# Two attention blocks in one program: new orders for the first block, and its later value loads cut into four

## The chip, the cores and the metric

The kernel runs on one core of a Trainium2 chip. The core has TensorE (PE; its weight loads are shown apart as PEld), VectorE (DVE), ScalarE (ACT), GpSimd (POOL) and SyncE (SP), which here only issues DMAs. The metric is device time in microseconds (us). The time before is a median of 1816.2 us over three runs (1811.39 to 1816.44).

## The reference

Two attention blocks A and B share one shape (2048 tokens, width 512, 32 heads of 16) and differ in the mask. A sees a window of 256 tokens, B sees every token. The outputs stand side by side.

```python
def _A_ref(x, wqkv, wo):
    B, S, D = x.shape
    H = 32; Dh = D // H; W = 256
    qkv = (x @ wqkv).reshape(B, S, 3, H, Dh).transpose(2, 0, 3, 1, 4)
    q, k, v = qkv[0], qkv[1], qkv[2]
    scores = jnp.einsum("bhqd,bhkd->bhqk", q, k) * (Dh ** -0.5)
    idx = jnp.arange(S)
    mask = (idx[:, None] - idx[None, :] >= 0) & (idx[:, None] - idx[None, :] < W)
    scores = jnp.where(mask[None, None], scores, -1e9)
    p = _softmax(scores, axis=-1)
    o = jnp.einsum("bhqk,bhkd->bhqd", p, v)
    return o.transpose(0, 2, 1, 3).reshape(B, S, D) @ wo
# _B_ref is the same without the mask
return jnp.concatenate([a, b], axis=-1)
```

## The kernel before, in words

**Work and stages.** The program has two stages. In the first stage (here: the first block), TensorE projects the queries, keys and values of A and of B, and does A's attention between them. In the second (the second block) it does B's attention and both output projections. Attention goes by units (b, g, c): block b, a group g of four heads, a chunk c of 512 queries. A has 8 groups by 4 chunks, so 32 units, and they run in that order. Two groups make a pair p.

**Kinds of work on TensorE in the first block.** Each has a letter in `ORDER_A` and a line in the profile:

- `p`: one projection tile of 128x512, 12 matmuls over all 128 rows of the array (L212).
- `g`: a quarter of two projection tiles at once. Each matmul is cut into halves of 64 rows that run beside each other, 12 matmuls a letter (L340); four letters, with other work between, make two tiles out of 48 matmuls.
- `m`: the scores of a tile without the maxima, whose row maxima VectorE takes (L505, then L514 and L515 on DVE). `e` is the same for B's first unit, ahead of time (L458).
- `t`: two small transposes (L582). They turn a unit's negated maxima into rows, which ScalarE copies out (L584) and a DMA puts beside the unit's queries (L589, `oq<-ntr`).
- `s`: the scores for real, of two heads (L615). ScalarE takes the exponentials (L622), GpSimd then zeroes what the mask hides (L632).
- `w`: the weights times the values (L661); the end of a unit is copied out by ScalarE (L672) and stored (L679).

**How parts of a projection travel.** A projected strip of queries or keys goes through ScalarE (L295, `raw`), then GpSimd writes its two parts into a tile `st` (L305 and L306; two such tiles take turns), and a DMA stores it to `parts` in HBM (L313, 512 KB). From there DMAs bring queries to `oq` (L386) and keys to `opk` (L370). Values go from ScalarE (L405) by `vst` to `vd` in HBM (L413) and come back into `vt` (L421): four loads of four tiles (272 KB) for the first pair of groups of A, and one load of 16 tiles (1088 KB) for each later pair.

**What sets the order.** `ORDER_P` lists the projections one by one (`Bk12` is block B, keys, pair 1, chunk 2). `ORDER_A` is the string of letters above. While the program is built, a planner walks through both with a model of the engines' time (`Model`). From that model's clock it decides where loads and the GpSimd and DVE work behind a projection are put between the letters: the lists "load", "k", "q", "v" hold what may be loaded, each with a condition and a time. On the chip nothing of the model is left. Each engine runs its own instructions in the order in which they were put, and waits on semaphores. All DMAs are issued by SP, one after the other, so a DMA that waits for its data holds all later ones.

Of the kernel before, what the change touches and what calls it, by code (L numbers as in the profile page):

```python
# [23 lines left out]
NQC = S // QC  # L24
# [24 lines left out]
FILL = 16  # L49
WARM = 22  # L50
ORDER_P = (
# [4 lines left out]
    "Bq21 Bq20 Bk33 Bq33 Bq22 Bq32 Bk32 Bk30 Bq11 Bq30 Bk31 Bq31 ").split()  # L56
WAKE = 200
LOAD = 105
LEAD = 1400
GAP = 3250  # L60
# [1 line left out]


ORDER_A = (
    "pppggppppmmggmmpppmgmmgmptmgmmgmpmmgsgmmpsmgmsgmmwtsgsmgmmpsmgsmgmmtwwpsmgsmgmswsmgsmgsmpmmswtwmsspm"
    "mswwsmgsmgsmwtmgmsgmgsmgmswsmgmsgmswsmgmsgmmtwmgmgmmpsmswtmsmwsswmmpssmwsmmpmstswmmspmswsmswsmmpmmsw"
    "tmswsmswsmmpmmspmswtmmmpsmswmmmpsmmwtmssmwmssmswmsmpmswsmmswtmsmwmsmssmwsmmpmmstwmswmsgmsgmswsmgmsgm"
    "mtwmswmssmwmsspmsmwtmsmswmsmmmpmsmwsmmswsmmtswmsmpmmswmtsmwsmssmmwsmpsmwmsmwmmpmsgsmgstwmsgsmgmmwtmm"
    "psmswwsmmpmsgmsgmswsgmgmtwsmgmsgmswgmsgmmwwtmsgmsgmswsmgmsgmgmsgmswsmgmsgmmtwwmsgsmgmswtmsgsmgsmwwms"
    "gmsgmswsmgsmgmtwmmpmmspsmswmmspmsmwsmsmwtmswsmmpmsmwsmsmwtsmswmsmpmsswmmswwmtmmpsmgmsgmswsmgsmgmwtes"  # L70
    "wmmmpmsgmmgstwesgesgmgsmgeswsmgsegeswmmmpmsmwsmwtmgesgmswsmgmsgempemmpmsmwtwemmpmsgsmgswesgsegmmwtms"
    "wmmmpsmgmsgeswsegsmgmswesgmsgeswsmgsmgmwsmmpmsmwwmmmpwtmmmp")
LAND = 700
LAND_V = 0
LGAP = 2500
EARLY = 2
# [3 lines left out]
class Model:  # L80
# [19 lines left out]
        return self.run("PE", turn + ns, *after)  # L100

    def dma(self, kb, *after):
        t = self.run("SP", {12: 800, 16: 600}.get(kb, 465), *after, self.lanes[0]) + 600
        self.t["DMA"] = max(self.t["DMA"], t) + int(3.4 * kb)

        self.lanes = [*self.lanes[1:], self.t["DMA"] + 1100]
        return self.lanes[-1]

    def bank(self, pool, n=0):

# [32 lines left out]
def attention_kernel(ctx: ExitStack, tc: tile.TileContext, xT, wqk, wv, wo, out):  # L143
# [12 lines left out]
    ns = 0  # L156
# [5 lines left out]
        eng.tensor_sub(t[:, 1], src, t[:, 0].bitcast(F32))  # L162

    slots_st, slots_v = [0, 0], [0, 0]
    staged = {"stage": [0] * 3, "p": [0] * 2 * AHEAD, "row": [0] * 2}

    def load_split(srcs, tags, d, keys, stage):

        slots = staged[stage]
        if stage == "p":  # L170
            r = sb.tile([128, 2, QC], F32, name=f"in_{keys[0]}".translate(NAMES), tag=stage, bufs=2 * AHEAD)
        else:
            r = sb.tile([128, QC], F32, name=f"in_{keys[0]}".translate(NAMES), tag=stage,
                        bufs=5 if stage == "row" else 3)[:, None]
        nc.sync.dma_start(r[:, :len(keys)], srcs)
        t = M.dma(256 * len(keys), slots.pop(0))

        def rest():
            for n, (tag, key) in enumerate(zip(tags, keys)):
                d[key] = sb.tile([128, 2, 512], F32R, name=f"{tag[0]}_{key}".translate(NAMES), tag=tag[0], bufs=tag[1])  # L180
                if key[:2] == (1, "o"):
                    nc.gpsimd.tensor_copy(d[key][:, 0], r[:, n])
                    nc.gpsimd.tensor_sub(d[key][:, 1], r[:, n], d[key][:, 0].bitcast(F32))
                    ready[tag[0], *key] = M.run("Pool", 2400, t)
                    continue
                split(r[:, n], d[key], nc.gpsimd if stage == "stage" else nc.vector)
                ready[tag[0], *key] = M.run(*(("Pool", 1260) if stage == "stage" else ("DVE", 602)),
                                            M.run("ACT", 500, t)) - LEAD * (stage != "stage")
            slots.append(ready[tag[0], *key])
        after(t + (LAND_X if stage == "stage" else 0), rest, (stage, *keys[0]))  # L190
# [94 lines left out]
    def end_qk(b, p, s, c, bank, ps):  # L285
# [11 lines left out]
            release(bank, t1)  # L297

        def sub():
            if (b, p) == (0, 0):  # L300
                nc.vector.tensor_sub(two[:, 1], ps, two[:, 0].bitcast(F32))
                t = M.run("DVE", 610, t1)
                release(bank, t)
            else:
                nc.gpsimd.tensor_copy(two[:, 0], raw)  # L305
                nc.gpsimd.tensor_sub(two[:, 1], raw, two[:, 0].bitcast(F32))  # L306
                t = M.run("Pool", 2000, t1)
            after(t, lambda: store(t), (project_qk, b, p, s, c))

        def store(t):  # L310
            if (b, p, s) not in parts:
                parts[b, p, s] = dram.tile([2, 128, S], F32, name=f"parts_{b}_{p}_{s}")
            nc.sync.dma_start(parts[b, p, s][:, :, c * QC:(c + 1) * QC].rearrange("p r t -> r p t"), two.bitcast(F32))  # L313
            ready["parts", b, p, s, c] = M.dma(512, t)
            slots_st.pop(0)
            slots_st.append(ready["parts", b, p, s, c])
        after(t1, sub, (project_qk, b, p, s, c))

    since = []
# [80 lines left out]
    def end_v(b, c, a, bank, ps):  # L400
# [2 lines left out]
        v = vst[0]  # L403
        vst.reverse()
        op = nc.scalar.activation(v[:, :, 0:DH], ps.rearrange("p (h d) -> p h d", d=DH), AF.Copy)  # L405
        t = mark(op, M.run("ACT", 480, M.t["PE"] + WAKE))
        release(bank, t)
        ready["vd", b, kt] = M.dma(272, t)
        slots_v.pop(0)
        slots_v.append(ready["vd", b, kt])  # L410
        if b not in vd:
            vd[b] = dram.tile([NG // 2, S, VP], F32, name=f"vd_{b}")
        nc.sync.dma_start(vd[b][:, kt * 128:kt * 128 + 128].rearrange("p t n -> t p n"),  # L413
# [6 lines left out]
    def load_v_now(b, p, k0, k1, t):  # L420
        nc.sync.dma_start(vt[p % 2][:, k0:k1, 0:VP],  # L421
                          vd[b][p, k0 * 128:k1 * 128].rearrange("(k t) n -> t k n", t=128))
        t = M.dma(68 * (k1 - k0), t, M.t["PE"])
        for kt in range(k0, k1):
            ready["v", b, p, kt] = t

# [526 lines left out]
    def load_q_at(b, g, c):  # L953
        load_q_now(b, g, c, ready["parts", b, g // 2, 0, c])

    def load_v_at(b, p, k0, k1):
        load_v_now(b, p, k0, k1, max(ready["vd", b, kt] for kt in range(k0, k1)))

    for u, (b, g, c) in enumerate(units[:NA + NQC]):
# [4 lines left out]
        elif c == 0:  # L964
# [40 lines left out]
    while todo_a or gen[0]:  # L1005
# [240 lines left out]
```

## Time and profile before

| What | Value |
|---|---|
| Median of three runs | 1816.2 us (1811.39 to 1816.44) |
| Profiled execution: its own time | 1817.04 us |
| Its span | 1815.3 us |
| First block ends (first matmul of L1167) | 530.72 us |
| Busy PE / DVE / ACT / POOL, us of the span | 1792.1 / 1508.8 / 1400.6 / 648.4 |
| Share of the DMA engines' time, queue q1, first 540 us | 62.4% |

A row of the timeline gives the start, the length, the engine, the line, the operation, what it writes and reads, how often, and in brackets the idle time before it with what ended that. A table of windows gives, for each stretch, its length, then the busy time of each engine with the number of its instructions, the granted TensorE clock, the DMA engines' share and GB/s. A row of the waits gives who waited for whom: the total in us, how often, and the longest.

### The profile page before, as it was taken

What the parts mean: (1) busy time and instruction counts of PE and PEld (TensorE: products, weight loads), DVE (VectorE), ACT (ScalarE), POOL (GpSimd) and SP (SyncE); (2) the same over time, 40 slices, a digit from 0 to 9 for tenths busy, and PEclk for the clock granted to TensorE, in tenths of its full rate; (3) what the DMA queues carried; (4) which work ended last, traced back from release to release, by engine and by line L of the source; (5) the groups of instructions that cost most, each with busy time, mean ns of one, the idle gap of its engine ahead of it and who ended that gap; (6) DMA issues with size and microseconds to landing.
All of it is one profiled execution on the core that took longest, in us unless ns stands there. A gap on an engine that the chain in (4) does not pass through costs nothing. (4 is left out here: it accounts for less than half of the span.)

```text
span 1815.3 us, 39121 instructions
## 1 busy us (share of the span) xinstructions
PE 1792.1 (99%) x15030; PEld 911.2 (50%) x15030; DVE 1508.8 (83%) x2243; ACT 1400.6 (77%) x2750; POOL 648.4 (36%) x1334
## 2 busy tenths in 40 slices
PE   9999899999999999999999999999999999999998
PEld 7776566767763555444444444444444434443436
DVE  4666676677779776899999999999999999999901
ACT  4366566665568776799999999999999999999983
POOL 0377777755755331033310024320112422022330
PEclk9999999999999999999999999999999999999999
DMA  8756566545572221311300211130031121010012
GB/s 264 208 182 212 186 190 211 179 139 170 181 202 97 77 86 65 83 30 47 65 17 31 56 49 29 29 78 16 16 76 35 29 63 37 17 54 14 25 37 93
DMA packets 129162, 166.80 MB, mean 92 GB/s; under 512 B 23012, under 2 KB 58852, under 8 KB 128964
## 3 DMA queue, kind: packets, MB, share of 16 engines
q1 hardware_dynamic: 128976, 164.31, 30.8%
q8 instruction: 118, 1.93, 0.5%
q14 instruction: 68, 0.56, 0.1%
HBM read 94.49 MB, written 68.19 MB: 90 GB/s over the span
## 5 line engine op out<-in xcount | busy, mean ns | idle before, releaser
L622 ACT ACTIVATE p<-ps_all 128x512 f32<-128x512 f32 x2432 | 1259.4, 597 | 185.5 <-PE ps_all L615 118.5
L462 DVE TENSOR_REDUCE mt<-ps_all 128x2 f32<-128x1024 f32 x1516 | 1195.3, 871 | 66.0 <-PE ps_all L458 59.2
L615 PE MATMUL ps_all<-oq,opk 51*128 51x512 f32 (+2 forms) x2752 | 773.3, 405 | 4.5 <-ACT p L622 2.1
L458 PE MATMUL ps_all<-opk,oq 48*128 48x512 f32 x2016 | 674.0, 438 | 0.2
L646 PE MATMUL ps_all<-p,vt 128*17 128x256 f32 (+1 forms) x6056 | 587.8, 460 | 0.5 <-ACT ou L672 0.5
L615 PEld LDWEIGHTS ps_all<-oq,opk 51*128 51x128 f32 x2752 | 398.0, 185 | 183.4 <-ACT p L622 157.4
L458 PEld LDWEIGHTS ps_all<-opk,oq 48*128 48x128 f32 x2016 | 308.4, 184 | 314.6 <-DVE mt L462 181.4
L632 POOL TENSOR_SCALAR_AFFINE_SELECT p<-p 128x256 f32<-128x256 f32 x480 | 178.9, 407 | 107.4 <-ACT p L622 107.0
L646 PEld LDWEIGHTS ps_all<-p,vt 128*17 128x17 f32 x6056 | 100.7, 95 | 223.4 <-issue 212.8
L532 POOL TENSOR_TENSOR mu<-mt 128x16 f32<-128x16 f32 x31 | 6.8, 220 | 503.9 <-DVE mt L462 503.9
L514 DVE COPY_PREDICATED ps_all<-mone,ps_all 128x256 f32<-128x256 uint16 x224 | 95.3, 425 | 95.3 <-PE ps_all L505 92.7
L515 DVE TENSOR_REDUCE nm<-ps_all 128x2 f32<-128x512 f32 x224 | 155.2, 693 | 7.7
L700 POOL TENSOR_TENSOR rd<-ld,minus 128x32 f32<-128x32 f32 x15 | 81.9, 5458 | 223.1 <-DMA ld<-od 223.1
L212 PE MATMUL ps_all<-x,w 128*128 128x512 f32 x432 | 112.9, 410 | 1.8 <-ACT x L161 1.2
L340 PE MATMUL ps_all<-x,w 64*128 64x512 f32 x672 | 112.8, 392 | 0.0
L661 PE MATMUL ps_all<-p,vt 128*17 128x384 f32 (+2 forms) x1408 | 96.2, 387 | 5.0 <-POOL p L632 5.0
L212 PEld LDWEIGHTS ps_all<-x,w 128*128 128x128 f32 x432 | 80.9, 194 | 27.4 <-issue 3.0
L295 ACT ACTIVATE raw<-ps_all 128x512 f32<-128x512 f32 x56 | 32.4, 597 | 80.3 <-PE ps_all L212 69.8
L212 PE MATMUL ps_all<-w_o,x_o 128*128 128x512 f32 x384 | 92.7, 396 | 1.0 <-ACT ob L765 1.0
L505 PE MATMUL ps_all<-opk,oq 48*128 48x384 f32 (+2 forms) x512 | 90.3, 367 | 2.4 <-DMA oq<-parts 0.6
L212 PEld LDWEIGHTS ps_all<-w_o,x_o 128*128 128x128 f32 x384 | 70.6, 188 | 30.8 <-issue 11.9
L340 PEld LDWEIGHTS ps_all<-x,w 64*128 64x128 f32 x672 | 80.1, 185 | 8.2
(77 smaller groups left out, 942.1 us busy)
## 6 DMA issues: line engine op xcount, KB each, us to landing
parts<-st SPq DMA_DIRECT2D x64, 512.0 KB
oq<-parts SPq DMA_DIRECT2D x128, 128.0 KB
opk<-parts SPq DMA_DIRECT2D x128, 128.0 KB
od<-ou SPq DMA_DIRECT2D x64, 256.0 KB
vd<-vst SPq DMA_DIRECT2D x32, 272.0 KB
oq<-parts SPq DMA_DIRECT2D x128, 64.0 KB
opk<-parts SPq DMA_DIRECT2D x128, 64.0 KB
t<-od SPq DMA_DIRECT2D x32, 256.0 KB
```

Source lines behind the costliest of these rows:

```text
L212: nc.tensor.matmul(ps, l(u), r(v), start=start and k == 0, stop=stop and k == n - 1)
L340: op = nc.tensor.matmul(view(banks[a ^ turn]), l(u)[rows], r(v)[rows], start=turn == q == 0, stop=turn == 1 and q == 11)
L458: nc.tensor.matmul(ps[:, n], q[rows, 128 * qt:128 * qt + 128], k[rows, kc * QC:kc * QC + QC], start=True, stop=True)
L462: op = nc.vector.tensor_reduce(out=m[:, a:a + len(heads), r, qt, kc], in_=ps, axis=AX.X, op=ALU.max)
L505: nc.tensor.matmul(two[:, a, 0:w], opq[b, g, c][rows, r, 128 * qt:128 * qt + 128], opk2(g)[rows, r, t0:t1], start=True, stop=True)
L514: nc.vector.copy_predicated(two[:, :, 256:384], later, two[:, :, 0:128])
L515: op = nc.vector.tensor_reduce(out=m[:, :, r, qt, 0], in_=two[:, :, 128:384], axis=AX.X, op=ALU.max)
L615: nc.tensor.matmul(ps[x][:, col:col + n1], opk2(g)[rows, pr, 128 * k:128 * k + 128], opq[b, g, c][rows, pr, q0:q0 + n1], start=True, stop= ...
L622: op = nc.scalar.activation(p[:, a0 + x, :w], ps[x][:, :w], AF.Exp, scale=SCALE)
L632: nc.gpsimd.affine_select(out=v, in_=v, pattern=[[0, 2], [sign, 128]], compare_op=ALU.is_ge, fill=zero_fill, base=base, channel_multiplier ...
L646: nc.tensor.matmul(o[32 * j:32 * j + VW, q0:q1], vt[(g // 2) % 2][:, kt, vc:vc + VW], pts[1, g, c, kt, j // 2][:, j % 2, q0:q1], start=kt ...
L661: nc.tensor.matmul(o[32 * j:32 * j + VW, q0:q0 + w], vt[(g // 2) % 2][:, kt, vc:vc + VW], pts[b, g, c, m, j // 2][:, j % 2, col:col + w], ...
```

## The change

Five things, all in what the planner is told or how it counts; no operation of the arithmetic is added or dropped.

1. `ORDER_P` and `ORDER_A` are replaced. `ORDER_A` goes from 50 `p` and 92 `g` to 48 `p` and 96 `g`; the other letters keep their numbers (280 `m`, 192 `s`, 96 `w`, 33 `t`, 16 `e`) and change places.
2. The later values come in four loads of four tiles instead of one of 16, each at least `GAP_V` behind the last by the model's clock.
3. `Model.dma` has a rate for each kind of transfer and another time to landing.
4. The GpSimd work that fills an `st` tile, and ScalarE's that fills a `vst` tile, wait in the model until the store that read this tile has landed.
5. `LAND` goes from 700 to 400 ns, and the early maxima's extra from 1500 to 500 ns.

```diff
+GAP_V = 1500
+PIECE = 4
-LAND = 700
+LAND = 400
     def dma(self, kb, *after):
-        t = self.run("SP", {12: 800, 16: 600}.get(kb, 465), *after, self.lanes[0]) + 600
-        self.t["DMA"] = max(self.t["DMA"], t) + int(3.4 * kb)
-        self.lanes = [*self.lanes[1:], self.t["DMA"] + 1100]
+        t = self.run("SP", {12: 800, 16: 600}.get(kb, 465), *after, self.lanes[0])
+        t, ns, land = (t - WAKE - 730, self.rate(kb) * kb, 2500) if self.load else (t + 600, 3.4 * kb, 1100)
+        self.t["DMA"] = max(self.t["DMA"], t) + int(ns)
+        self.lanes = [*self.lanes[1:], self.t["DMA"] + land]
         return self.lanes[-1]
+    def rate(kb):
+        if kb % 257 == 0 or kb % 69 == 0:
+            return 3.98 if kb % 257 else 3.47
+        return {12: 0, 16: 0, 256: 1.87, 272: 3.19, 300: 4.71, 512: 3.0}.get(kb, 4.16)
...
         def sub():
+            slot = landed["st"].pop(0) if landed["st"] else 0
...
-                t = M.run("Pool", 2000, t1)
+                t = M.run("Pool", 2000, t1, slot)
...
     def load_v_at(b, p, k0, k1):
+        gapv[0] = M.t["PE"] + GAP_V
         load_v_now(b, p, k0, k1, max(ready["vd", b, kt] for kt in range(k0, k1)))
...
-                list_("v", lambda u=u: done["w"] >= u - 2 * NQC and (u < NA or ne == len(early)),
-                      lambda b=b: max(ready.get(("vd", b, kt), NEVER) for kt in range(NT)), load_v_at, b, g // 2, 0, NT)
+                for k0 in range(0, NT, PIECE):
+                    list_("v", lambda u=u: done["w"] >= u - 2 * NQC and (u < NA or ne == len(early)),
+                          lambda b=b, k0=k0: max(gapv[0] if k0 else 0, *(ready.get(("vd", b, kt), NEVER)
+                                                                          for kt in range(k0, k0 + PIECE))),
+                          load_v_at, b, g // 2, k0, k0 + PIECE)
...
         elif x == "e":
-            t = max(ready.get(("qe",), NEVER), ready.get(("ke", early[ne][2]), NEVER)) + LAND + 1500
+            t = max(ready.get(("qe",), NEVER), ready.get(("ke", early[ne][2]), NEVER)) + LAND + 500
```

What the engines are given. **SP, the value load of A's third pair.** These are SP's rows before. `vt0<-vd_0` is the value load of all 16 tiles, `parts<-st` the store of a projected strip, `in_1_1` an input strip of B, `ld` a small load.

```order
L679 DMA od_0_0_3_1633<-ou_0_1_3_2384 128x512
L421 DMA vt0_77<-vd_0_319 128x16x136
L313 DMA parts_0_3_0_2209<-st_0_3_0_3_2290 128x2x512
L175 DMA in_1_1_0_2424<-xT_B 128x512
L693 DMA ld_0_0_3_2440<-od_0_0_3_1633 128x1x32
L313 DMA parts_0_2_1_947<-st_0_2_1_3_2355 128x2x512
```

And SP's rows at this place of the change:

```order
L692 DMA od_0_0_3_1614<-ou_0_1_3_2391 128x512
L434 DMA vt0_77<-vd_0_261 128x4x136
L324 DMA parts_0_2_1_2073<-st_0_2_1_2_2294 128x2x512
L434 DMA vt0_77<-vd_0_261 128x4x136 x2
L185 DMA in_1_1_0_2435<-xT_B 128x512
L706 DMA ld_0_0_3_2441<-od_0_0_3_1614 128x1x32
L398 DMA oq_0_3_0_2450<-parts_0_1_0_1408 16x2x512
L398 DMA oq_0_3_0_2450<-parts_0_1_0_1408 32x2x512
```

The store that stood behind 16 tiles now stands behind four; eight come behind it, and the last four behind the query load and one more store.

**GpSimd at the same place**, before. `p_0_2_0_2` are the two weight tiles of the third step of unit (0,2,0), which its last `w` reads; `st` are the strips' parts.

```order
L632 AFFINE_SELECT p_0_2_0_2_0_2428<-p_0_2_0_2_0_2428 128x2x128
L305 CAST st_0_3_1_1_2421<-raw_0_3_1_1_2422 128x512
L306 TENSOR_TENSOR st_0_3_1_1_2421<-raw_0_3_1_1_2422,st_0_3_1_1_2421 128x512
L632 AFFINE_SELECT p_0_2_0_2_1_2466<-p_0_2_0_2_1_2466 128x2x128
L632 AFFINE_SELECT p_0_2_1_0_0_2481<-p_0_2_1_0_0_2481 128x2x128 x3
```

And in the change:

```order
L645 AFFINE_SELECT p_0_2_0_2_0_2404<-p_0_2_0_2_0_2404 128x2x128
L171 TENSOR_TENSOR x_1_0_3_2416<-in_1_0_3_2281,x_1_0_3_2416 128x512
L645 AFFINE_SELECT p_0_2_0_2_1_2446<-p_0_2_0_2_1_2446 128x2x128
L316 CAST st_0_2_1_1_2432<-raw_0_2_1_1_2433 128x512
L317 TENSOR_TENSOR st_0_2_1_1_2432<-raw_0_2_1_1_2433,st_0_2_1_1_2432 128x512
L645 AFFINE_SELECT p_0_2_1_0_0_2475<-p_0_2_1_0_0_2475 128x2x128 x3
```

The second tile's mask stood behind the strip's cast and now stands ahead of it.

**SP, the third query strip of A's first pair**, before, from its store to its load (`one_d` are constant rows, `in_0_1_0` and `in_0_1_1` weights):

```order
L313 DMA parts_0_0_0_199<-st_0_0_0_2_359 128x2x512
L313 DMA parts_0_0_1_231<-st_0_0_1_2_424 128x2x512
L413 DMA vd_0_319<-vst0_79 128x4x136
L270 DMA one_d_82<-vt1_78 768x1x16
L360 DMA opk0_75<-one_d_82 3x4096 x2
L360 DMA opk1_76<-one_d_82 3x4096 x2
L175 DMA in_0_1_1_448<-wqk_A 128x512
L386 DMA oq_0_0_2_454<-parts_0_0_0_199 16x2x512
```

And in the change:

```order
L324 DMA parts_0_0_0_199<-st_0_0_0_2_499 128x2x512
L426 DMA vd_0_261<-vst1_80 128x4x136
L324 DMA parts_0_0_0_199<-st_0_0_0_3_545 128x2x512
L185 DMA in_0_2_1_569<-wqk_A 128x512
L398 DMA oq_0_0_2_601<-parts_0_0_0_199 16x2x512
```

The strip is projected later, so its load stands four rows behind its store where it stood nine DMAs behind it. The second block keeps its order on TensorE, row for row.

More of the change, by code (lines that the diff above doesn't have):

```diff
@@ L64 @@
 ORDER_A = (
[L65 to L72, printed above, removed]
-LAND = 700
+    "ppppppppppmmpmmpmgmgmmpmtgmmgmpsmgmsgmmpmsgmsgmmtwsgmsgmmpmsgsmgmmtwwmmpsmgmsgmswwmsgmsgmmpmsstwsmpg"
+    "smgmswsmgmsgmmwsgmgsmtwsmgsmgmmwwtmsgmsgmswsmgmsgmswmmmpssmtwwmspmsmwssmgsmgsmwtmsgsmgmwsmswssmwmmmp"
+    "msmtwssmwmsmpsmmpsmwtmmmpsmswmsmpmsmwsmmswwtmsmsmsmpmsmtwsmsmwsmmswmsswmmspsmmwmswtmsgsmgsmwmsgsmtgm"
+    "mwsmwsmmswsmsmpsmmwmswtmsmwsmmmpmsssmmwsmsmwtmmmpsmswmsmsmwtsmsmwmsmpmsmwmstwmmmpmsgmsgmswmmgswtsmgm"
+    "mpssmwwmsgsgmpsgmsgmmwwsgmsgmstwmsgmsgmmwwtsmgmsgmswsmgmsgmgsmgmstwmsgmmgmwmswsmgmsgmswtmsgmsgsmwwsm"
+    "gsmgmswsmgsmgsmtwwmmmpmsmpmmswsmsmwtmsgsmgmswsmgmsgsmwmsmtwsmmswmsswmmmpmsmswtswmmmpsmgsmgsmwwmsgsmg"
+    "etwmmmpmsgmsgmswsmgesgegsmgeswsmgsegemtwmmpmsmwmswsegsmgmstwmsgmsgempemmpmsmwwtemmpmsgmsgsmwmgesgesw"
+    "mmmpesswtmgesgmswsmgmgmswsmgsmgsewmgsmgmswemspsmmwwtmmmpmmmwp")
+LAND = 400
 LAND_V = 0
@@ L299, in sub @@
         def sub():
+            slot = landed["st"].pop(0) if landed["st"] else 0
             if (b, p) == (0, 0):
                 nc.vector.tensor_sub(two[:, 1], ps, two[:, 0].bitcast(F32))
-                t = M.run("DVE", 610, t1)
+                t = M.run("DVE", 610, t1, slot)
                 release(bank, t)
@@ L405, in end_v @@
         op = nc.scalar.activation(v[:, :, 0:DH], ps.rearrange("p (h d) -> p h d", d=DH), AF.Copy)
-        t = mark(op, M.run("ACT", 480, M.t["PE"] + WAKE))
+        t = mark(op, M.run("ACT", 480, M.t["PE"] + WAKE, landed["v"].pop(0)))
         release(bank, t)
@@ L410, in end_v @@
         slots_v.append(ready["vd", b, kt])
+        landed["v"].append(slots_v[-1])
         if b not in vd:
```

10 lines of the change are left out of this document (7 added, 3 removed), and 8 rows, old and new, of the table ORDER_P.

## The prediction

> **What bounds the kernel now.** I read the busy time of the engines first, then the table of windows, then the waits of TensorE, then the timeline around its longest wait.
>
> ```profile
> PE 1792.1 (99%) x15030; PEld 911.2 (50%) x15030; DVE 1508.8 (83%) x2243; ACT 1400.6 (77%) x2750; POOL 648.4 (36%) x1334
> 20.00:60.00 40.00, 39.54 (x232) 31.64 (x229) 22.37 (x52) 11.86 (x22) 1.29 (x1) 1.00 0.79 216
> 100.00:190.00 90.00, 89.89 (x828) 62.70 (x820) 61.09 (x143) 56.42 (x115) 70.12 (x133) 1.00 0.66 204
> 190.00:220.00 30.00, 23.82 (x207) 13.69 (x205) 17.92 (x52) 18.69 (x39) 20.91 (x39) 0.89 0.68 217
> 220.00:270.00 50.00, 47.83 (x410) 31.37 (x412) 35.45 (x87) 32.31 (x66) 39.25 (x79) 0.93 0.56 169
> 270.00:320.00 50.00, 47.66 (x440) 31.74 (x436) 31.88 (x78) 30.53 (x63) 36.59 (x63) 1.00 0.67 208
> 320.00:531.00 211.00, 210.20 (x2003) 150.04 (x1998) 153.82 (x286) 121.72 (x244) 138.32 (x278) 1.00 0.54 172
> 531.00:1815.00 1284.00, 1277.31 (x10531) 548.24 (x10529) 1152.19 (x1480) 1097.09 (x2144) 318.67 (x690) 1.00 0.18 50
> ```
>
> TensorE is busy in 99% of the span, so the first block can get shorter only by less work on TensorE or by less waiting of it. The first number after the length of a stretch is TensorE's busy time. It lacks 6.2 us in 190 to 220, 2.2 in 220 to 270 and 2.3 in 270 to 320: 10.7 us in 130 us. In 100 to 190 and from 320 on it lacks under 1 us each. The two stretches with a clock below 1.00 are those with the longest waits. The second block, 1284 us, keeps its order on TensorE, and I leave its time as it is.
>
> The longest wait has a chain, seen in three timelines (SP, POOL, PE):
>
> ```profile
> 190.76 0.39 SPq L421 DMA_DIRECT2D vt<-vd  x1
> 191.24 2.14 SPq L313 DMA_DIRECT2D parts<-st  x1
> 199.78 0.61 POOL L305 CAST st<-raw 128x512 fp32r<-128x512 f32 x1 [6.05 <-DMA parts<-st]
> 201.69 1.48 POOL L632 TENSOR_SCALAR_AFFINE_SELECT p<-p 128x256 f32<-128x256 f32 x4
> 202.15 1.04 PE L661 MATMUL ps_all<-p,vt 128*17 128x256 f32 x4 [4.60 <-POOL p L632]
> ```
>
> SP sends the value load of 1088 KB and right behind it a store of 512 KB. The store's landing frees an `st` tile, for which GpSimd sits 6.05 us in its cast. Behind the cast in GpSimd's queue stands a mask, and TensorE waits 4.60 us for that.
>
> **Term 1, fewer turns.** Counted in the program's order, TensorE changes between the kinds of work (whole-array projections; row halves, maxima and scores; values and transposes) 264 times in the first block before and 246 times after.
>
> ```profile
> 23.05 5.60 PE L212 MATMUL ps_all<-w_v,x 128*128 128x512 f32 x24
> 28.49 2.88 PE L212 MATMUL ps_all<-x,w 128*128 128x512 f32 x12
> 32.30 3.05 PE L340 MATMUL ps_all<-w_v,x 64*128 64x512 f32 x24
> 35.08 0.51 PE L505 MATMUL ps_all<-opk,oq 48*128 48x256 f32 x4
> 35.52 3.01 PE L212 MATMUL ps_all<-x,w 128*128 128x512 f32 x12
> 38.37 5.60 PE L212 MATMUL ps_all<-w_v,x 128*128 128x512 f32 x24
> 43.90 0.44 PE L505 MATMUL ps_all<-opk,oq 48*128 48x384 f32 x2
> ```
>
> From start to start, 24 projection matmuls with no turn take 28.49 - 23.05 = 5.44 us, so 12 take 2.72. Twelve that follow a turn take 38.37 - 35.52 = 2.85, so this turn costs 0.13. Twenty-four that end in a turn take 43.90 - 38.37 = 5.53, so that one costs 0.09. I take 0.11 for each, also for the turns to the values, which no row prices alone: 18 x 0.11 = 2.0 us, with 0 and, at twice the price, 4.0 as ends. One pair of projection tiles also goes from whole rows to row halves: 24 halves take 35.08 - 32.30 = 2.78 us, 48 take 5.56, against 5.44: +0.1. Together **-1.9 us**.
>
> **Term 2, the wait at 197.5 us.** In the change the store stands behind 272 KB where it stood behind 1088, and on GpSimd the mask of (0,2,0) that the 4.60 us were spent on stands ahead of the strip's cast. Both links of the chain are cut, so I take off the whole **-4.6 us**. Late next are the masks of unit (0,2,1), which still stand behind a cast; this cast waits for a store behind 272 KB, so I charge a quarter of 4.6: **+1.1 us** (ends 0 and 4.6).
>
> **Term 3, the clock.** The granted clock drops in two places:
>
> ```profile
> 200.00:210.00 10.00, 7.85 (x46) 5.08 (x46) 3.58 (x12) 3.40 (x7) 7.91 (x17) 0.66 0.50 163
> 250.00:260.00 10.00, 9.48 (x56) 6.25 (x54) 6.44 (x19) 4.38 (x10) 5.92 (x11) 0.66 0.71 219
> 204.59 4.17 PE L212 MATMUL ps_all<-x,w 128*128 128x512 f32 x12
> 251.65 1.01 PE L505 MATMUL ps_all<-opk,oq 48*128 48x384 f32 x4 [0.48 <-ACT p L622]
> 252.59 5.49 PE L212 MATMUL ps_all<-x,w 128*128 128x512 f32 x12
> ```
>
> Each loses 34% of 10 us, so 3.4 us of clock. The first follows the 4.60 us wait; TensorE was idle in its first 2 us, which leaves some 2.4 us of loss; the 12 matmuls that take 4.17 us instead of 3.01 lie in it. I take **-2.4 us**, since the wait goes. The second has 12 matmuls at 5.49 instead of 3.01, a loss of 2.5, and no wait over 0.5 us just ahead of it. What set it off I cannot tell; the order differs here, so I take half: **-1.2 us** (ends 0 and -2.5).
>
> The page "TensorE: Matmul & The Clock Gate" of the Trainium skill, section "Why this matters for your kernels", says that idle gaps over about 3 us between bursts drop the clock. The first stretch agrees, with its 4.60 us; the second does not, with 0.48. By that rule alone the second loss would not hang on this change's waits, and the sum below would be 1.2 us smaller.
>
> **Term 4, the third pair's sequel at 297 us.**
>
> ```profile
> 297.36 0.38 SPq L421 DMA_DIRECT2D vt<-vd  x1
> 297.84 5.60 SPq L386 DMA_DIRECT2D oq<-parts  x4
> 303.54 0.38 SPq L313 DMA_DIRECT2D parts<-st  x1
> 312.71 0.73 PE L340 MATMUL ps_all<-w_v,x 64*128 64x512 f32 x4 [1.13 <-POOL w_v L162]
> ```
>
> Here the next value load is followed by a query load that keeps SP for 5.60 us, and the strip's store goes out only at 303.54. Of the 2.3 us that TensorE loses up to 320, 1.13 are one wait for GpSimd. The change puts the store ahead of that query load and the value load on both sides of it in halves. I take half of 2.3: **-1.1 us** (ends 0 and -2.3).
>
> **Term 5, what gets tighter.** The third query strip of A's first pair is projected later. Counted in TensorE's order, 210 matmuls stood between its projection and its first maxima, and 98 do now (24 whole, 48 halves, 26 others). By the rows above those are 5.4 + 5.6 us, and with some 0.09 a piece for the 26 and ten turns at 0.11, 14.4 us. What has to fit into it:
>
> ```profile
> 21.86 0.36 SPq L313 DMA_DIRECT2D parts<-st  x1
> 23.62 1.86 SPq L386 DMA_DIRECT2D oq<-parts  x4
> 25.53 3.90 SPq L370 DMA_DIRECT2D opk<-parts  x4
> SPq L370 <- DMA parts<-st: 2.1, 2, 1.9
> 32.13 0.41 PE L505 MATMUL ps_all<-opk,oq 48*128 48x128 f32 x3 [0.21 <-DMA opk<-parts]
> L291 ACT ACTIVATE st<-ps_all 128x512 fp32r<-128x512 f32 x8 | 4.8, 595 | 6.0 <-PE ps_all L212 2.8 <-DMA parts<-st 2.5 <-ACT vst L405 0.7
> L301 DVE TENSOR_TENSOR st<-ps_all,st 128x512 fp32r<-128x512 f32 x8 | 5.5, 687 | 3.2 <-ACT st L291 3.2
> ```
>
> The key load that ends at 29.43 waited up to 1.9 us for a store of 21.86, so a store takes up to some 7 us; from that load's end to the maxima that wait for it are 2.7; the four query loads take 1.86 on SP; and the strip's two evictions, 0.595 and 0.687 us, lie ahead of the store. That is 13 of 14.4 us in the densest DMA stretch (share 0.79). I charge **+1.0 us** (ends 0 and 3.9, as long as SP was held in the row of 3.90).
>
> **Term 6, twelve more DMA issues** (16 for four in the first block).
>
> ```profile
> L421 SPq DMA_DIRECT2D vt<-vd x11: 359/424/512, 60.6 to 1329.2; - x11
> ```
>
> 12 x 0.424 = 5.1 us of SP's time. SP waits at most of these places for data anyway, and the values are needed only when the next pair's units come, so I count **0** (upper end 5.1, if SP is the bound there).
>
> **Sum.** -1.9 - 4.6 + 1.1 - 2.4 - 1.2 - 1.1 + 1.0 = -9.1 us. The profiled execution has 1817.04 us, 1.7 outside its span, and lies 0.8 above the median, 1816.2. On its own time that gives 1807.9, on the median 1807.1. I forecast **1807 us**.
>
> The page "DMA: Bandwidth & Descriptors" of the Trainium skill, section "Rules for kernel authors", speaks against the cut: it asks for 1 MiB or more per DMA and for many transfers to be made one. No row here shows the cost beyond the issue time; the third rival is what it would do.
>
> **The rivals.** *The waits only move* (17%). GpSimd keeps its work, and it is busy for 70.12 of the 90 us up to 190. If another cast meets a late store within a few masks of a `w`, a wait like 4.60 and its clock loss come back elsewhere: -9.1 + 4.6 + 2.4 = -2.1, so 1814 us. For it: static distances between a strip's store and the next cast are about as short as before around 270 us and shorter after 430. Against it: three of the four large value loads made no wait near 4 us.
>
> *The rows come late in every unit* (slower, 12%). `LAND` lets scores be put 300 ns closer behind their rows (`oq<-ntr`).
>
> ```profile
> PE ps_all L615 <- DMA oq<-ntr: 0.9, 2, 0.5
> SPq L589 <- ACT ntr L584: 22.1, 9, 7.1
> ```
>
> In the eighth tightest of 32 units 57 matmuls stand between transposes and first scores, where 61 stood. Before, only two scores waited, for 0.9 us. The point from which this decides is 9.1 / 32 = 0.28 us a unit: there the gain is gone. At 0.5 us a unit it is 16 - 9.1 = +6.9, so 1823 us. Against it: the margin shrinks by about what 0.3 us is, and 0.9 us in all says that most units had more.
>
> *The cut loads cost SP's time* (7%). All 5.1 us of term 6 are exposed at the places where SP is behind: -4.0, so 1812 us.
>
> **How the numbers follow.** A measurement of this kernel can tell 0.3%, 5.4 us, from no change. My forecast has 64%. Faster by over 0.3% (below 1810.8): the forecast's 64%. Within 0.3%: the first and third rival, 24%. Slower by over 0.3%: the second, 12%. Low end: all ends in favour, -3.9 - 4.6 - 2.4 - 2.5 - 2.3 = -15.7, and the rest of the waits in 220 to 270, -2.2, some 18 us: 1798, and I take 1797. High end: the second rival at 0.4 us a unit, +3.7: 1820. I leave out 7% below and 10% above.
>
> **What would show each step.** Term 1: as many matmuls, 264 turns down to 246, and windows without waits that are shorter. Terms 2 and 3: around 190 to 200 us no POOL cast with an idle time near 6 us ahead of it, no wait of a `w` (L661) near 4.6, and a granted clock of 1.00 through the first block. Term 4: no query load of 5 us ahead of a strip's store near 290. Term 5: a wait of L505 for `oq<-parts` around 60 us. Second rival: many waits of L615 for `oq<-ntr`. The forecast is wrong if the second block's length moves by over 3 us, or if POOL's waits for `parts<-st` (10.5 us in the first block before) stay or grow:
>
> ```profile
> POOL st L305 <- DMA parts<-st: 10.5, 4, 6.1
> ```

## The result and the profile after

The changed kernel takes 1805.64 us (median of six runs, 1803.28 to 1808.07) where the kernel before took 1816.32 (six runs, 1811.39 to 1823.25): a ratio of 0.9939, 95% interval 0.9916 to 0.9963. In a later series of six and 18 runs it was 0.9947 (0.9927 to 0.9966). The forecast was 1807, in 1797 to 1820.

The profiled execution took 1803.61 us, with a span of 1801.9, against 1817.04 before. First block first, from the table of windows of before (stretch, its length, then the busy time of PE, PEld, DVE, ACT and POOL, the granted clock, DMA share, GB/s):

```profile
0.00:530.72 530.72, 514.54 (x4498) 362.71 (x4499) 356.62 (x763) 303.19 (x607) 329.44 (x645) 0.99 0.63 194
```

And the windows of the changed kernel, with the stretches of the prediction, cut at its own end of the first block:

```profile
0.00:517.78 517.78, 507.06 (x4522) 360.38 (x4523) 356.81 (x763) 301.69 (x604) 328.21 (x642) 1.00 0.64 198
20.00:60.00 40.00, 37.52 (x199) 28.90 (x199) 19.65 (x48) 10.63 (x20) 0.00 (x0) 1.00 0.80 221
190.00:220.00 30.00, 27.40 (x253) 17.10 (x255) 20.92 (x57) 20.54 (x41) 25.73 (x50) 0.94 0.75 229
220.00:270.00 50.00, 48.54 (x457) 30.78 (x453) 39.94 (x94) 36.35 (x75) 42.01 (x83) 1.00 0.64 189
270.00:320.00 50.00, 50.00 (x485) 36.33 (x485) 31.48 (x79) 30.68 (x63) 40.97 (x71) 1.00 0.70 220
518.00:1801.90 1283.90, 1278.27 (x10532) 547.99 (x10530) 1152.65 (x1480) 1098.33 (x2147) 322.74 (x692) 1.00 0.19 50
```

The first block ends 12.9 us earlier and the second block keeps its length (1283.9 us, 1284.0 before). That the second stays equal is partly chance: at 524.5 us it now holds a half-rate stretch (3.41 us in which the granted clock is 0.5), where it held none, and TensorE idles 5.6 us in it, 6.7 before. Clear of the clock it got some 1.8 us shorter. The two profiled executions also lie 13.4 us apart, the medians 10.7, so a part of the 12.9 us belongs to this pair. Of the 12.9 us, 16.18 - 10.72 = 5.5 are idle time of TensorE (length minus busy time of the block), and 514.54 - 507.06 = 7.5 are busy time for the same work. 190 to 220 lacks 2.6 us (6.2 before), 220 to 270 lacks 1.5 (2.2), 270 to 320 nothing (2.3). But 20 to 60 lacks 2.5, where it lacked 0.5.

The chain at 190 us looks like this in the timelines of SP, POOL and PE of the changed kernel:

```profile
191.59 0.42 SPq L434 DMA_DIRECT2D vt<-vd  x1
192.11 0.52 SPq L324 DMA_DIRECT2D parts<-st  x1
192.69 1.73 SPq L434 DMA_DIRECT2D vt<-vd  x2
194.64 0.41 POOL L645 TENSOR_SCALAR_AFFINE_SELECT p<-p 128x256 f32<-128x256 f32 x1
197.73 0.61 POOL L316 CAST st<-raw 128x512 fp32r<-128x512 f32 x1 [2.68 <-DMA parts<-st]
198.80 0.50 PE L628 MATMUL ps_all<-oq,opk 51*128 51x384 f32 x4 [0.57 <-ACT p L635]
199.46 4.61 PE L222 MATMUL ps_all<-x,w 128*128 128x512 f32 x12
```

The store (192.11) stands behind one short value load, the mask (194.64) ahead of the cast, and the cast waits 2.68 us where it waited 6.05. Of these 3.4 us less, 1.3 are that GpSimd comes to the cast later (at 195.05, 193.73 before), with other work done first. No `w` waits for a mask. What is left on TensorE are waits of half a microsecond for ScalarE's exponentials. The projection at 199.46 takes 4.61 us and not 3.0: a half-rate stretch of the clock is still there. The two stretches of ten microseconds of the prediction now read:

```profile
200.00:210.00 10.00, 9.18 (x73) 5.93 (x71) 5.08 (x24) 6.00 (x13) 9.69 (x23) 0.83 0.90 277
250.00:260.00 10.00, 9.46 (x83) 6.03 (x82) 7.42 (x28) 7.99 (x16) 7.92 (x17) 1.00 0.58 182
```

The waits in the first block (who waited for whom, sum, times, longest):

```profile
POOL st L316 <- DMA parts<-st: 12.7, 9, 2.7
PE ps_all L628 <- ACT p L635: 2.4, 5, 0.6
PE ps_all L518 <- DVE st L312: 1.3, 1, 1.3
PE ps_all L628 <- issue: 1.2, 1, 1.2
```

GpSimd waits longer for stores in all, 12.7 us (10.5 before), but in nine waits of at most 2.7 and not four of up to 6.1. The last two rows are new, at 36.5 and 58.3 us: they are the loss in 20 to 60.

A reading aid for what follows: runs of one and the same program differ by 3 to 14 us, and the granted clock differs with them. A half-rate stretch that takes 0.1% off the mean clock makes a run some 1.8 us longer. So each series also has the mean of (time x granted clock), which is an estimate of the time without these stretches; the differences in the table below have standard errors of 0.4 to 0.8 us. In the last series before has 1807.0 and the changed kernel 1800.4: 6.6 us of the gain are waits and work, and the rest, some 3, is clock.

### The profile page after: what moved, and what is told of

The parts are those of the page before. It is cut to its first block, busy times and chain, and to the rows that moved or that the text cites. A ratio compares the mean times of both kernels' runs of the same rounds, so it can differ in the third digit from the quotient of the medians.

```text
span 1801.9 us, 39175 instructions
## 1 busy us (share of the span) xinstructions
PE 1785.6 (99%) x15054; PEld 908.6 (50%) x15054; DVE 1509.5 (84%) x2243; ACT 1400.2 (78%) x2750; POOL 651.0 (36%) x1334
## 5 line engine op out<-in xcount | busy, mean ns | idle before, releaser
L352 PE MATMUL ps_all<-x,w 64*128 64x512 f32 x744 | 125.9, 392 | 0.0
L222 PE MATMUL ps_all<-x,w 128*128 128x512 f32 x396 | 101.4, 405 | 2.1 <-ACT x L170 1.5
L352 PEld LDWEIGHTS ps_all<-x,w 64*128 64x128 f32 x744 | 89.8, 185 | 9.6 <-issue 0.4
L222 PEld LDWEIGHTS ps_all<-x,w 128*128 128x128 f32 x396 | 73.1, 191 | 24.3 <-issue 2.7
```

The source lines that it names most:

```text
L222: nc.tensor.matmul(ps, l(u), r(v), start=start and k == 0, stop=stop and k == n - 1)
L352: op = nc.tensor.matmul(view(banks[a ^ turn]), l(u)[rows], r(v)[rows], start=turn == q == 0, stop=turn == 1 and q == 11)
```

## The experiments

Theory: the gain comes from the chain at 197 us, from fewer turns and from the waits around 300 us. Rivals: one part of the change makes it all (the cut loads, the orders, or the planner), the waits only move, or the gain is in the clock.

### The three parts, alone and in pairs

The change was taken apart into the orders (`ORDER_P`, `ORDER_A`), the four loads (`PIECE`, `GAP_V`) and the planner (rates, waits for `st` and `vst` tiles, `LAND`). All corners beside the kernel before, each against the runs of before in its own series:

| Orders | Loads | Planner | Ratio to before (95%) | Time x clock, us against before |
|---|---|---|---|---|
| old | four | old | 0.9981 (0.9968 to 0.9994) | -3.0 |
| new | one | old | 0.9994 (0.9985 to 1.0004) | +0.5 |
| old | one | new | 1.0016 (1.0003 to 1.0029) | +0.2 |
| new | four | old | 0.9968 (0.9952 to 0.9985) | -2.1 |
| new | one | new | 0.9968 (0.9952 to 0.9983) | -3.8 |
| old | four | new | 0.9984 (0.9968 to 0.9999) | -1.7 |
| new | four | new | 0.9947 (0.9927 to 0.9966) | -6.6 |

**Four loads alone:**

```diff
+PIECE = 4
-    list_("v", ..., load_v_at, b, g // 2, 0, NT)
+    for k0 in range(0, NT, PIECE):
+        list_("v", ..., load_v_at, b, g // 2, k0, k0 + PIECE)
```

> The kernel before with only the later value loads cut into four (old orders, old model). Theory (two links make the 4.6 us wait near 197 us: the store behind 1088 KB, and the mask behind the cast; either link cut shortens it): the wait of the values' matmuls for GpSimd there falls from 4.6 us to under 2, the clock loss at 200 us goes or halves, first block 4 us shorter (2 to 7), so about 526.5 us to the first matmul of the second block. Rival (the new orders alone bring the gain, the cut is worth nothing): the wait stays over 4 us, first block within 1.5 us of 530.7.

The profiled first block ended at 525.6 us. In its timelines of POOL and PE:

```profile
197.57 0.61 POOL L307 CAST st<-raw 128x512 fp32r<-128x512 f32 x1 [2.81 <-DMA parts<-st]
199.95 0.88 PE L663 MATMUL ps_all<-p,vt 128*17 128x256 f32 x4 [1.64 <-POOL p L634]
```

And in its table of windows:

```profile
200.00:210.00 10.00, 9.69 (x54) 6.35 (x54) 3.88 (x14) 4.31 (x8) 6.53 (x16) 0.66 0.72 233
```

The cast waits 2.81 us instead of 6.05, and the `w` 1.64 instead of 4.60: a shorter load ahead of the store takes 3 us off the chain, as the theory had it, in one profile of each kernel. The clock of the stretch behind it is 0.66 all the same.

**New orders, one load, new planner:**

```diff
-PIECE = 4
+PIECE = 16
```

> The changed kernel with the later value loads whole again (one of 1088 KB each; new orders, new model). Theory: the mask still stands ahead of the cast, so no wait near 4.6 us comes back; GpSimd's cast waits longer (over 4 us once) and TensorE loses 1 to 3 us more than the changed kernel, first block 519 to 521 us. Rival (the cut carries the gain): first block over 523 us and a wait over 3 us near 190 us.

Its first block ended at 521.1 us, at the upper end of the theory's range. GpSimd's waits there:

```profile
POOL st L316 <- DMA parts<-st: 14.4, 8, 5.3
```

The longest, 5.28 us, is the cast's near 197 us, and yet TensorE has no wait over 0.7 us from 190 to 215. So the order on GpSimd cuts the chain too, without the short loads.

**New orders alone:**

```diff
-    "Aq00 Ak00 Ak01 Av10 Av01 Aq01 Av02 Av21 Aq02 Ak02 Av33 Av32 Av00 Ak03 Av03 Aq03 Av11 Av13 Av20 Ak20 Aq11 "
+    "Aq00 Ak00 Ak01 Av01 Av00 Av03 Aq01 Av02 Ak02 Av11 Av23 Av31 Aq03 Av30 Aq02 Ak03 Av20 Av10 Av12 Av21 Ak11 "
...
-    "pppggppppmmggmmpppmgmmgmptmgmmgmpmmgsgmmpsmgmsgmmwtsgsmgmmpsmgsmgmmtwwpsmgsmgmswsmgsmgsmpmmswtwmsspm"
+    "ppppppppppmmpmmpmgmgmmpmtgmmgmpsmgmsgmmpmsgmsgmmtwsgmsgmmpmsgsmgmmtwwmmpsmgmsgmswwmsgmsgmmpmsstwsmpg"
...
```

> The kernel before with only the two new orders (old model, whole loads, old LAND). Theory: turns (about -3 us with all kinds of turn) and the mask ahead of the cast carry most of it: first block 519 to 523 us. Rival (the model's placing of loads and the cut carry it): first block over 525 us.

The profiled block ended at 522.5 us, inside the theory's range, but 11 runs gave 0.9994: no gain that can be measured. The one profile caught a short run, and here it misled. No `w` waits near 197 us in this run, so the orders alone cut the chain too. What eats the gain are other waits, as far as this one profile shows them. The longest, from 57.3 us on, is ahead of the first scores, where the changed kernel waits 1.2. PE's waits have it as:

```profile
PE ps_all L615 <- issue: 2.5, 1, 2.5
```

Three more are rows of PE's timeline in this run:

```profile
296.63 0.50 PE L340 MATMUL ps_all<-x,w 64*128 64x512 f32 x1 [1.04 <-DVE nm L515]
467.96 1.65 PE L340 MATMUL ps_all<-x,w 64*128 64x512 f32 x12 [0.68 <-ACT p L622]
485.98 1.66 PE L340 MATMUL ps_all<-x,w 64*128 64x512 f32 x12 [1.32 <-DVE mt L462]
```

**New orders, four loads, old planner**, so the run above with

```diff
+PIECE = 4
+GAP_V = 1500
```

> The new orders and the four loads with the old model: no rates by kind, no wait for an st or vst tile, LAND 700 and 1500. Theory (the new model's placement is worth some 4 us beside the other two parts): the first block ends between 520.5 and 524 us, and the median is 3 to 6 us above the changed kernel's. Rival (the orders and the cut loads are all of the gain): the first block ends between 517 and 519 us.

It ended at 525.3 us, later than both expected, and its ratio, 0.9968, lies 0.0021 above the changed kernel's, some 3.8 us, as the theory had it. The two intervals overlap; by time x clock the distance is 4.5 us. PE's timeline has the same three waits at the same places of the program:

```profile
299.52 0.49 PE L342 MATMUL ps_all<-x,w 64*128 64x512 f32 x1 [1.04 <-DVE nm L517]
470.71 1.65 PE L342 MATMUL ps_all<-x,w 64*128 64x512 f32 x12 [0.68 <-ACT p L624]
488.71 0.49 PE L342 MATMUL ps_all<-x,w 64*128 64x512 f32 x2 [1.32 <-DVE mt L464]
```

With the new planner, in the changed kernel and with one load, PE has no wait over 0.3 us from 285 to 500 us. So 3.0 us of what the planner brings to the new orders are these three waits.

**The planner on the old orders**, with four loads (the changed kernel with the first lines of the orders, and all that follow, put back) and with one:

```diff
-    "Aq00 Ak00 Ak01 Av01 Av00 Av03 Aq01 Av02 Ak02 Av11 Av23 Av31 Aq03 Av30 Aq02 Ak03 Av20 Av10 Av12 Av21 Ak11 "
+    "Aq00 Ak00 Ak01 Av10 Av01 Aq01 Av02 Av21 Aq02 Ak02 Av33 Av32 Av00 Ak03 Av03 Aq03 Av11 Av13 Av20 Ak20 Aq11 "
...
```

> The changed kernel with ORDER_P and ORDER_A of before: the new model and the four loads on the old orders. Theory (the planner's placement is a gain of its own): the wait near 197 us is under 1 us, TensorE's visible idle time in the first block is under 10 us, and the first block ends under 523 us (525.6 with the four loads alone). Rival (the placement pays only with the orders that were made for it): the first block ends within 1.5 us of 525.6 or later, and the median is within 1.5 us of that run's.

```diff
-PIECE = 4
+PIECE = 16
```

> The last corner of the grid: the orders of before, one value load for each later pair, and only the new model (rates, waits for st and vst tiles, LAND). Theory (the new model helps the orders that were searched on it, and not the old ones): median within 3 us of before, first block between 526 and 532 us. Rival (the wait for an st tile in the model moves the cast behind the masks by itself, as in the run with one cast later): no wait of a w over 1.5 us near 197 us, first block under 524 us.

With four loads the first block ended at 521.7 us and the wait near 197 was 0.44, as the theory of that run had it; TensorE's idle time in the block was 10.6 us, where the theory had under 10. But the ratio, 0.9984, is that of the loads alone within the noise, and time x clock gained 1.7 us where the loads alone gained 3.0. So the one profile's block speaks against the rival and the runs speak for it: the planner adds nothing there that can be measured. With one load the kernel is slower, 1.0016 (4.0 us by the medians, where I expected at most 3, and a block of 534.4 us where I expected up to 532). By time x clock it is level with before (+0.2), so this loss is mostly clock. Its PE and POOL timelines have the old chain nearly whole:

```profile
200.97 0.61 POOL L316 CAST st<-raw 128x512 fp32r<-128x512 f32 x1 [6.07 <-DMA parts<-st]
203.34 1.04 PE L674 MATMUL ps_all<-p,vt 128*17 128x256 f32 x4 [4.41 <-POOL p L645]
```

The wait for a tile in the model does not by itself move this cast behind the masks. What follows from the table: by time x clock the three parts alone add up to -2.3 us, all three together make -6.6. The orders gain 4.0 and 4.9 us with the new planner (one load, four loads) and nothing with the old one, so they pay only with the planner that places the loads and casts between their letters. This rests on time x clock: by the plain ratios the new orders with four loads and the old planner, 0.9968, could also be better than the four loads alone, 0.9981, as the intervals overlap. Which part of the planner does it (rates, waits for tiles, `LAND`) was not taken apart.

### One cast moved

The kernel before, with one strip's cast held back in the planner:

```diff
-        after(t1, sub, (project_qk, b, p, s, c))
+        after(t1 + (2500 if (b, p, s, c) == (0, 3, 1, 1) else 0), sub, (project_qk, b, p, s, c))
```

> The kernel before with one piece of GpSimd work moved: the cast of the strip (A, pair 3, keys, chunk 1) 2.5 us later in the planner, so that it stands behind the masks that it stood ahead of. Theory: the wait of 4.6 us near 197 us falls to under 1.5 us and the half clock at 200 us goes, first block 4 to 6 us shorter. Rival (the cast's wait is only handed to the next masks): the wait stays at 3 us or more, one mask later, and the first block is within 1.5 us of 530.7.

Ratio 0.9968 (0.9956 to 0.9979), time x clock 4.0 us lower; the profiled block ended at 521.3 us, 9.4 earlier, more than expected. (The planner also put some later loads elsewhere.) POOL's and PE's timelines at the place:

```profile
192.80 1.12 POOL L632 TENSOR_SCALAR_AFFINE_SELECT p<-p 128x256 f32<-128x256 f32 x3 [0.38 <-ACT p L622]
197.80 0.61 POOL L305 CAST st<-raw 128x512 fp32r<-128x512 f32 x1 [3.88 <-DMA parts<-st]
200.24 0.29 PE L505 MATMUL ps_all<-opk,oq 48*128 48x128 f32 x1 [0.72 <-DMA oq<-parts]
```

And its table of windows:

```profile
200.00:210.00 10.00, 8.78 (x68) 4.53 (x72) 3.36 (x18) 5.68 (x12) 9.91 (x23) 0.59 0.66 200
```

The masks stand ahead of the cast, the cast still waits 3.88 us, and nobody waits for it: the 4.60 us are gone. By time x clock this one line gives 4.0 us, where the whole change gives 6.6. But the clock from 200 to 210 is 0.59, lower than before, with no wait over 0.72 us. The part of the theory that tied the half rate at 200 us to the one long wait fell.

Both links cut on the old orders, this cast and the four loads:

```diff
+PIECE = 4
+GAP_V = 1500
-        after(t1, sub, (project_qk, b, p, s, c))
+        after(t1 + (2500 if (b, p, s, c) == (0, 3, 1, 1) else 0), sub, (project_qk, b, p, s, c))
```

> The kernel before with both links of the chain at 197 us cut and nothing else: the four loads, and the one strip's cast behind the masks. Theory (both cure the same wait, so they don't add up): the first block ends between 520 and 523 us, and the median lies 6 to 9 us under before, as with the cast alone. Rival (they add up, as the loads also save SP time elsewhere): the first block ends under 519 us, and the median lies 10 us or more under before, so the new orders would not be needed for the gain.

Ratio 0.9963 (0.9947 to 0.9979), time x clock 2.8 us lower, against 4.0 and 3.0 for each alone. The median lies 6.5 us under before, in the theory's range; the one profiled block ended at 526.6 us, outside it. They cure the same wait and don't add up, and by time x clock 3.8 us of the whole change are left for the new orders with their planner.

### The price of a turn

Behind the warm-up of the changed kernel stands a block of matmuls on constant operands (so its span, 1848.0 us, says nothing). An `f` is one matmul over the whole array (128*128, 128x512), an `h` a pair of row halves (64*128, 64x512), a `c` four value matmuls (128*17, 128x256). Ahead of what the diff shows stand 36 `f`, 12 `h` and 12 `c` by themselves:

```diff
+        for _ in range(12):
+            f()
+            h()
+        for _ in range(12):
+            f()
+            c()
+        for _ in range(12):
+            h()
+            c()
```

> The changed kernel with a block of extra matmuls on constant operands behind the warm-up: 36 over the whole array (f), 12 pairs of row halves (h), 12 sets of four 17-column value matmuls (c), and then 12 times f h, 12 times f c, 12 times h c in turn. It measures what a turn costs. Theory of the prediction: 0.11 us a turn, so each of the three alternating stretches takes 24 x 0.11 = 2.6 us more than its 12 + 12 matmuls do by themselves. Rival: about 0.2 us a turn, so 4.8 us more in each; then 18 turns fewer are worth 3.6 us and not 2.0. The program is some 35 to 45 us longer than the changed kernel, and that length says nothing else.

In PE's timeline of its one execution, the 24 halves by themselves, the 48 value matmuls by themselves (the profile has two records of each, so 96), and then the first rows of the three alternating stretches and the first behind them:

```profile
14.71 3.04 PE L355 MATMUL ps_all<-opk 64*128 64x512 f32 x24
17.68 5.37 PE L359 MATMUL ps_all<-vst,vt 128*17 128x256 f32 x96
22.98 0.51 PE L350 MATMUL ps_all<-opk 128*128 128x512 f32 x1
33.37 0.50 PE L350 MATMUL ps_all<-opk 128*128 128x512 f32 x1
45.22 0.50 PE L355 MATMUL ps_all<-opk 64*128 64x512 f32 x2
57.06 5.29 PE L222 MATMUL ps_all<-x,w 128*128 128x512 f32 x22
```

From start to start, 12 h take 17.68 - 14.71 = 2.97 us and 12 c 22.98 - 17.68 = 5.30, each with one turn in it; 12 f take 2.72, as in the prediction. The stretch f h takes 33.37 - 22.98 = 10.39 us, so 23 more turns cost 10.39 - 2.72 - 2.97 = 4.70: 0.20 us each. The stretch f c takes 11.85, and 11.85 - 2.72 - 5.30 = 3.83 for 23 turns: 0.17. The stretch h c takes 11.84: 3.57 for 22, so 0.16. A turn costs 0.16 to 0.20 us, nearer the rival's 0.2 than the prediction's 0.11.

### Two letters moved

The changed kernel, to fill the waits at 58 and 197 us:

```diff
-mmpmtgmmgmpsmgmsg
+mmpmtgmmgmpmgsmsg
-wwtmsmsmsmpmsm
+wwtmsmpsmsmmsm
```

> The changed kernel with two letters of ORDER_A moved: the first scores stand behind a quarter g instead of ahead of it, and a projection p stands between the scores at 197 us instead of behind them. Theory: the waits of 1.17 us at 58 us (rows that land late) and of 0.59 and 0.57 us at 197 us go, since TensorE has other work there, and the first block ends at 517.8 - 2.3 = 515.5 us, between 514.5 and 516.5. Rival (the waits only move, as the planner puts other loads to the new clock): waits of the same sum elsewhere, and the first block ends between 517 and 520 us.

The theory was wrong, and the rival too mild: the ratio to before is 0.9981 (0.9968 to 0.9994), where the changed kernel has 0.9947, and the profiled block ended at 527.2 us, past the rival's 520. The waits did not keep their sum: TensorE idles 15.3 us in this block, 10.7 in the changed kernel's. PE's timeline shows where a wait went:

```profile
64.16 0.41 PE L628 MATMUL ps_all<-oq,opk 51*128 51x384 f32 x4
64.41 0.39 PE L518 MATMUL ps_all<-opk,oq 48*128 48x384 f32 x2
65.97 0.51 PE L628 MATMUL ps_all<-oq,opk 51*128 51x384 f32 x4 [1.17 <-ACT p L635]
200.94 3.02 PE L222 MATMUL ps_all<-x,w 128*128 128x512 f32 x12 [0.59 <-ACT p L635]
```

The first scores no longer wait, but the next ones wait just as long for ScalarE; and the projection that was to fill the wait at 197 us waits itself.

### Eight loads, and the changed kernel again

```diff
-PIECE = 4
+PIECE = 2
```

> The changed kernel with PIECE = 2, so eight loads of 136 KB for each later pair where it has four of 272 KB. Theory (four are enough, since no store's wait decides any more, and eight only add 16 issues of 0.42 us in the first block): first block within 2 us of 517.8, median within 2 us of the changed kernel's or up to 4 above. Rival (the shorter block ahead of stores is what pays): POOL's waits for parts<-st in the first block fall under 9 us (12.7 with four), and the first block ends under 515.5 us.

Median 1808.45 us, 3.6 above the changed kernel in the same series, as the theory allowed, and time x clock 5.1 us above it: this program costs time. The block ended at 521.4 us, 3.6 behind 517.8, which the theory did not allow. GpSimd's waits for stores in the first block fell:

```profile
POOL st L316 <- DMA parts<-st: 8.0, 5, 2.9
```

So the rival's condition came true without its effect. Whether the loads cost by themselves, or by what the planner puts elsewhere because of them, is not shown.

> The changed kernel itself, beside the three that follow on one chip. Theory: its gain is in waits and turns, which every run has, and only a part of it in half-rate stretches of the clock, which come and go from run to run; then each run's time multiplied by its own granted clock lies 6 to 8 us under that of before, and the plain median 9 to 12 us. Rival: the gain is mostly of the clock, and the product is less than 4 us lower.

Time x clock 6.6 us and the plain median 10.3 us under before, both in the theory's range. The profiled execution was a long one, 524.4 us for the first block. POOL's and PE's timelines show that the wait for the store is nearly back:

```profile
196.26 0.40 POOL L645 TENSOR_SCALAR_AFFINE_SELECT p<-p 128x256 f32<-128x256 f32 x1
201.78 0.61 POOL L316 CAST st<-raw 128x512 fp32r<-128x512 f32 x1 [5.12 <-DMA parts<-st]
204.96 0.64 PE L518 MATMUL ps_all<-opk,oq 48*128 48x128 f32 x2 [1.00 <-DVE rd L718]
209.21 1.07 PE L628 MATMUL ps_all<-oq,opk 51*128 51x128 f32 x4 [2.18 <-DMA oq<-ntr]
```

The cast waits 5.12 us, and no `w` waits for it, since the mask went ahead at 196.26. Instead the rows of a unit come 2.18 us late. None of the kernels tried beats the changed one.

## Why the prediction was right, point by point

**The bound.** The second block kept its length, 1284.0 and 1283.9 us, but only with a half-rate stretch that it had not before; clear of it, some 1.8 us of the gain lie there, for which I had no term. And one reading was off: I wrote that the stretches with a clock below 1.00 are those with the longest waits. 220 to 270 has no wait over 0.53 us; 270 to 320, at a clock of 1.00, has one of 1.13.

**Term 1 (turns, -1.9 us)** was mis-sized. Of the turns 82 lay between whole rows and halves before and 76 lie there now, 179 and 169 between halves and columns, 3 and 1 between whole rows and columns. At the measured 0.20, 0.16 and 0.17 that is, as an estimate from constant operands, 1.2 + 1.6 + 0.3 = 3.1 us, and with the +0.1 of the halves -3.0. The profile agrees within 0.7 us: of the 7.5 us less busy time some 3.8 are clock (term 3), and 3.7 are left. The step that was off is the price of one turn. My rows showed 0.13 us in the matmuls behind a turn and 0.09 in those ahead of one, and I took their mean. The experiment has f to h 0.44 from start to start and h to f 0.43, where an f or an h by itself takes 0.23: each turn costs both parts together, 0.20.

**Term 2 (-4.6 + 1.1).** The wait went, by both links, and each cuts it by itself: the shorter load ahead of the store 3 us of it, the mask ahead of the cast all of it. The first link is the weaker one. Behind a long load the cast waited 3.88 to 6.07 us in four programs, behind a short one 2.06 to 2.81 in four, but 5.12 in the second execution of the changed kernel. The +1.1 for the masks of (0,2,1) did not come; two waits for ScalarE, 0.59 and 0.57 us, stand in its place, so the net was right by chance and its carrier wrong.

**Term 3 (clock, -3.6).** The size held in this pair of profiles and its reason failed, so that it held is luck. Before, the two stretches lost 6.8 us of clock; TensorE was idle for 2.7 us of them, which at half rate is 1.3, so 5.5 us of work were lost. After, 17% of 10 us, 1.7: -3.8 in these two profiles. But I wrote that the first loss goes "since the wait goes". With the wait gone, the half rate still lies at 200 us in the changed kernel, and longer in the run with one cast moved (3.41 and 10.24 us, 6.83 before). The rule of the Trainium skill that I weighed there (the page "TensorE: Matmul & The Clock Gate", section "Why this matters for your kernels": idle gaps over about 3 us drop the clock) does not account for these stretches either, with no wait over 0.72 us near them. Over all runs of the last series the mean clock went from 0.9953 to 0.9967, some 2.5 us. What the stretches do follow stands at the end.

**Term 4 (-1.1)** was half of what came: 270 to 320 lost 2.3 us and loses nothing. Its reason, the store put ahead of the query load, is not shown: with the long loads and the old orders, and only one cast moved, that stretch loses nothing either (TensorE busy for 50.00 of 50 us).

**Term 5 (+1.0)** was the right stretch and the wrong place: 20 to 60 us loses 2.0 us more, but not at the third strip's maxima. One wait is for VectorE's release of a bank (36.5 us), the other ahead of the first scores (58.3). In SP's timeline the rows of these scores are issued at 52.25 us, and with the scores moved later that wait went.

**Term 6 (0)** held for four loads: the loads alone were no loss. The program with eight lost 5.1 us of time x clock. The advice of the Trainium skill (the page "DMA: Bandwidth & Descriptors", section "Rules for kernel authors": 1 MiB or more per DMA for the most bandwidth) is so not borne out by loads of 272 KB here. The run with 136 KB goes its way, without showing that the size is the reason.

**The sum** was -9.1; the medians say -10.7 and -10.3. Without the clock I had -5.5, and the runs -6.6. In part the sum came so close because errors cancel: terms 1 and 4 were each some 1.1 us too small, and term 5, a loss, 1.0.

**The rivals.** "The waits only move" was wrong for this change, and too mild for the two letters. "Rows late in every unit" was wrong as a whole, but its mechanism exists: 2.18 us at one unit, in one profiled execution of the same program. Four loads in place of one did not cost. One criterion was bad: I wrote that the forecast is wrong if GpSimd's waits for `parts<-st` grow. They grew from 10.5 to 12.7 us, and TensorE got faster, because the masks no longer stand behind the long ones.

## What to carry to other kernels

Ask of a wait on an engine off the path who stands behind it in its queue, and not how long it is: one mask moved ahead of one cast gave 4.0 us by itself, where the whole change gave 6.6. An order that was searched against a planner belongs to this planner; taken alone, the orders gave nothing. And where runs of one program differ by more than the effect, take many runs and each run's granted clock, since a single profile of the orders alone showed 8 us that were not there.

## What the runs showed of the hardware

- Half-rate stretches of TensorE's clock come in multiples of 3.41 us, and their number differs between executions of the same program: 3.4 us of the first block in one profile of the changed kernel, 17.1 in the other. In seven of the 13 profiles without the extra matmuls one began between 199 and 202 us, with longest waits from 4.60 down to 0.59 us in the four microseconds ahead of it.
- Where they begin is not random, though the cause is not shown. In all 14 profiles they lie on a grid of 3.41 us that starts where the clock first rises, 4.0 to 7.2 us into the span. I added up, for each full-rate interval of the grid, rows times columns that TensorE streams, with 12 whole-array matmuls in 2.72 us as 1 (an estimate from the traces; matmuls beside each other add, so it can pass 1). Its median is 1.09. All 34 half-rate stretches before the end of a program stand right behind one of the 98 emptiest of 7342 intervals, below 0.62. The other 64 of these have none behind them. Such an interval need not be idle: ahead of the stretch at 251.46 us of the kernel before, TensorE was busy for 2.85 of 3.42 us. No run varied this alone.
- A turn between matmuls of the whole array, of row halves and of 17 columns costs 0.16 to 0.20 us, a part of it ahead of the turn and a part in the row that follows it.
- The same store at the same place of the same program let GpSimd wait 2.68 us in one execution and 5.12 in another.
